# A fused attention and two-MLP kernel: the first eight weight chunks at a lower rank, first operands in one transfer, and another cost of an issue in the schedule

## The chip, the cores and the metric

The kernel runs on one core of a Trainium2 chip. The metric is the device time of one execution in microseconds (us). A core has five engines, each with an instruction queue of its own that it works through in order: TensorE (PE in the profile; PEld is its load of the stationary operand, which runs beside the products), VectorE (DVE), ScalarE (ACT), GpSimd (POOL) and SyncE (SP), which in this kernel does nothing but issue the DMA transfers. An instruction waits on semaphores for the results of other engines and of transfers.

## What is computed

```python
def _attn_ref(q, k, v):                 # B=4, H=8, S=576, D=64
    scores = scale * np.matmul(q, k.transpose(0, 1, 3, 2))
    mask = block_i >= block_j           # blocks of 64 positions
    scores = np.where(mask, scores, -1000000000.0)
    attn = softmax(scores)
    return np.matmul(attn, v)

def _moe_ref(x, w1, w2, w3, w_out):     # x is 2304 x 512, w1..w3 are 512 x 768
    h = np.maximum(np.maximum(x @ w1, x @ w2), x @ w3)
    return h @ w_out

def _moe2_ref(x, w_in, w_out):          # w_in is 512 x 2048
    h = np.maximum(x @ w_in, 0.0)
    return h * h @ w_out

def reference(...):                     # heads are put side by side in between
    return _moe2_ref(_moe_ref(_attn_ref(q, k, v)))
```

q, k and v are 32-bit floats. The weights of both MLPs are 64-bit floats and come to the chip as such.

## The kernel before, in words

**Stages.** The 32 heads are worked on as 16 pairs n (four batches of four pairs, NPAIR = 4). A pair has two groups of query rows, g = 0 (the first 256) and g = 1 (the other 320). For each, TensorE forms scores (sc) from the operands (zk for group 0 of the first four pairs, z and k for their group 1, qs, kh, kl for later pairs), VectorE masks them and takes the negated maximum (nm), ScalarE forms the exponentials (P) with their sums (sm), TensorE transposes them (tp), ScalarE or VectorE copies the transposes out (ta, tb), TensorE multiplies with v (av) and spreads the reciprocal sums over rows (r), which ScalarE copies out (rs). The result, x, is split in two halves of shorter numbers, xh and xl.

The first MLP (`mlp1(b, g)`) multiplies x of one batch and group with w1, w2 and w3, in six columns c of 128 by three i: tiles l, with running maximum run; then h, split in hh and hl, with w_out (also named l, from wo1h and wo1l), copied to ys and written to y_d. Every product is three products of halves: low times high, high times low, high times high. The second MLP follows, in a later stage with other buffers: y is loaded (yf), multiplied with the rearranged second weights wq into ph (p is its copy, c and g the activations), and g with wol and woh into acc.

**Weights.** `load_w_` takes one chunk of 128 rows by 512 numbers: a transfer of 512 KB (raw_w, raw_wo or raw_wi, in 64 bits), two conversions on ScalarE, a shift and a bit operation on VectorE, a sum on GpSimd, a cast to the high half on ScalarE (w1h) and a subtraction on VectorE (w1l). The first MLP has 18 chunks of w1 to w3, named raw_w_c_i, and six of w_out (raw_wo_0 to raw_wo_5). `with_weights` deals them out among the attention steps of batch 0. In the second MLP the chunks become tiles wqf, then wq, which is written to wq_d (1792 KB each) and loaded again later.

**What sets the order.** The code only notes operations. `Plan.issue` then chooses, one at a time, the engine and operation with the earliest start by its own tables of durations (`duration`, `transfer`); of those that could start at the same time on an engine, the one of the lowest rank goes first, then the one noted first. A chunk of the first weights has rank 0 as the attention does, mlp1 has rank 1, the second weights 2. The result is a fixed order on each engine, and on SyncE a fixed order of transfers. There are eight DMA queues used in turn, so an issue also waits for the transfer issued eight before it.

The operands of group 0 of a pair n < 4 are one tile zk of 128 by 3 by 256: z of head 0, z of head 1, and k, brought by three transfers of 128 KB in `score_operands_f32`. Two such tiles exist.

Of the kernel before, what the change touches and what calls it, by code (L numbers as in the profile page):

```python
# [24 lines left out]
NPAIR = H // 2  # L25
# [15 lines left out]
GA, GB = 256, 320  # L41
# [3 lines left out]
CFG = dict(PD=-1, PE=1, A1=0, A2=0, WP=1, FC=(8, 16), WO=55, FI=0, LO2=0, HI2=0, Q2=0, RN=3, XL=2, HL=2, SO=0, TF=0, W_A=0.7, W_B=1.5, SPARE='hl..rhl..rhl..r..r..r', S=15, PB=3, QB=(2, 2, 3), BANKS=(3, 2, 1, 2), LO=0, HI=0, Q=0, EV=('*', '*'), EV2=('a', 'a'), CB=2, PC=0, PM=1000, PX=-0.5, PO=0, HH='*', XH='*', N0='a', YS='a', HIS=0, RB=1, TB=(2, 1), KB=1, CT='a', LT='d', XA=4, XB=0)  # L45
# [123 lines left out]
class Plan:  # L169
# [56 lines left out]
    def issue(self):  # L226

        ops, free, held, queue = self.ops, self.free, self.held, self.queue
        left = [0 for op in ops]
        users = [[] for _ in ops]  # L230
        for op in ops:
            for d in (*op.deps, *op.after):
                if d.end is None:
                    left[op.index] += 1
                    users[d.index].append(op)
        waiting = {e: {} for e in free}

        def offer(op):
            for e in op.engines:
                when = 0.0  # L240
                for d in op.deps:
                    when = max(when, d.end + ((SEM[d.engine] + (500 if e == 'pe' else 0)) if d.engine != e else 0))
                waiting[e][op.index] = when, shares_port(e, op)

        for op in ops:
            if not left[op.index]:
                offer(op)
        for _ in ops:
            best = None
            for e, w in waiting.items():  # L250
                if not w:
                    continue
                other = held["pool" if e == "dve" else "dve"] if e in held else 0.0
                start = {i: max(free[e], at, other if port else 0.0) for i, (at, port) in w.items()}
                t = min(start.values())
                i = min((i for i, s in start.items() if s <= t), key=lambda i: (ops[i].rank, i))
                if best is None or t < best[0]:
                    best = t, e, i
            t, e, i = best
            op = ops[i]  # L260
            op.engine = e
            length = duration(e, op) * SLOW[e]
            if e in held and waiting[e][i][1]:
                held[e] = t + length - HOLD[e]
            for other in op.engines:
                del waiting[other][i]
            if e == "sp":
                queue = max(t + 1500, queue) + transfer(op)
                op.end, free[e] = queue + 400, t + 60
            else:  # L270
                op.end = t + length
                free[e] = op.end - LAP[e]
            for tile in op.makes:
                tile.make()
            self.tc.keep_in_program_order(self.call(self.real[e], alias(e, op.name), op.args, op.kw))
            for u in users[i]:
                left[u.index] -= 1
                if not left[u.index]:
                    offer(u)
        self.ops, self.queue = [], queue  # L280
# [15 lines left out]
def width(x):  # L296
    return math.prod(x.area.shape[1:])


def alias(engine, name):  # L300
    return {"act": "copy", "dve": "tensor_copy"}.get(engine, name) if name in ("copy", "tensor_copy") else name


def shares_port(engine, op):
    if engine not in ("dve", "pool"):
        return False
    sources = [x for k, x in op.kw.items() if k.startswith("in") and isinstance(x, View) and not x.psum]
    if engine == "pool" or len(sources) > 1:
        return bool(sources)
    return bool(sources) and not op.kw["out"].psum and width(op.kw["out"]) % 2 == 0 and op.name != "tensor_reduce"  # L310


def duration(engine, op):
    views = op.views()
    n = max(map(width, views))
    psum = any(x.psum for x in views)
    if engine == "pe":
        stat, mov = op.args[1:] if op.args[1:] else (op.kw["lhsT"], op.kw["rhs"])
        if op.name == "transpose":
            return 109  # L320
        n, m = width(op.args[0]), width(stat)
        if stat.tile.args[1] == F32:
            return (4 * n / 2.4 + 5) * (0.5 if m == 64 else 1)
        return max(n, 230) / 2.4 + (11 if n < 300 else 13)
    if engine == "act":
        if op.name == "activation" and "accum_out" in op.kw:
            return 455 + 0.834 * n
        return (160 if psum else 200) + 0.82 * n
    if engine == "pool":
        return 140 + 2.25 * n  # L330
    if engine == "sp":
        return 60
    if op.name == "memset":
        return 60 + n
    if op.name == "reciprocal":
        return 150 + 6.4 * n
    if op.name in ("tensor_scalar", "tensor_copy", "copy") and not psum:
        return (200 if isinstance(op.kw.get("scalar1"), View) else 150) + n / 1.92
    return 157 + n / 0.96


def transfer(op):
    x = next(v for v in op.views())
    return 128 * 4 * width(x) / 320.0


@with_exitstack
def fused_kernel(ctx: ExitStack, tc: tile.TileContext, z0, k0, qk, v, w123, wo1, win2, wo2, out):
    nc = Plan(tc)
    mm = nc.tensor.matmul  # L350

# [23 lines left out]


    def load_w(src, hi, lo, name):
        with nc.ranked(CFG["PC"]):
            load_w_(src, hi, lo, name)

    def load_w_(src, hi, lo, name, f=None):
# [42 lines left out]
    chunks = []  # L424
# [61 lines left out]
    def score_operands_f32(n, g):  # L486


        a, w = GROUPS[g] if n < NPAIR else (0, S)
        if n < NPAIR and g == 0:  # L490
            zk = at.tile([128, 3, GA], F32, tag="tb", bufs=2 * CFG["TB"][1], name=f"zk{n}")
            z, k = [zk[:, h] for h in range(2)], zk[:, 2]
        else:
            z = [at.tile([128, w], F32, tag=t, bufs=CFG["QB"][2 * (t == "kl")], name=f"z{n}_{t}") for t in ("qs", "kl")]
            k = at.tile([128, S], F32, tag="kh", bufs=CFG["QB"][1], name=f"k{n}")
        nc.sync.dma_start(out=z[0], in_=z0[n, :, 0, a:a + w])
        nc.sync.dma_start(out=k, in_=k0[n, :, :a + w])
        nc.sync.dma_start(out=z[1], in_=z0[n, :, 1, a:a + w])
        return [[(z[h], k)] for h in range(2)], None

    def value_operands(n, g):
# [279 lines left out]
    with nc.behind(marks[CFG["WO"]][0]), nc.ranked(2):  # L781
        for m in (m for q in range(NQ) for m in (q, q + NQ)):
            t = at.tile([128, 2, DM], F32R, tag="wos", name=f"wos{m}")
# [265 lines left out]
```

## Time and profile before

| what | value |
| --- | --- |
| median of 3 runs | 888.12 us (883.44 to 889.05) |
| profiled execution: time | 888.7 us |
| profiled execution: span | 886.9 us |
| mean granted clock of TensorE | 0.995 of full |
| TensorE busy | 864.2 us (97%) |
| VectorE busy | 601.1 us (68%) |
| ScalarE busy | 424.9 us (48%) |
| GpSimd busy | 104.0 us (12%) |

All times in rows come from the profiled execution and count from the start of its span. Busy shares are means over the whole span; the stages differ, so they are read stage by stage.

### The profile page before, as it was taken

How to read it: one execution, taken by the hardware profiler on the slowest of the kernel's cores; microseconds unless marked ns; L12 is line 12 of the kernel's file. 1: busy time of each engine (PE TensorE's matmuls, PEld its weight loads, DVE VectorE, ACT ScalarE, POOL GpSimd, SP SyncE). 2: the span in 40 equal slices, each digit the busy share in tenths (PEclk: the TensorE clock that was granted, in tenths of full speed). 3: DMA queues.
4: the chain of work that ended last, by engine and by line, in shares of the span. 5: the costliest groups of instructions: out<-in, count | busy, mean ns of one | idle time of the engine just before them, and what ended most of it. 6: DMA issues, size and time to landing. Idle time of an engine off the chain costs nothing.

```text
span 886.9 us, 14852 instructions
## 1 busy us (share of the span) xinstructions
PE 864.2 (97%) x5464; PEld 777.7 (88%) x5464; DVE 601.1 (68%) x1376; ACT 424.9 (48%) x1016; POOL 104.0 (12%) x94
## 2 busy tenths in 40 slices
PE   5899999999999999999999989999999999999997
PEld 4567799998999989899999979898999989999896
DVE  6998678878788988646557766546755457544543
ACT  6888667667688787544555231113211114211111
POOL 2233200000001111214442230000000000000000
PEclk9999999999999999999999999999999999999999
DMA  8745432232255563554656578454765536655221
GB/s 294 237 138 174 131 114 89 85 115 86 85 184 177 175 213 118 196 190 165 257 203 237 164 299 338 160 230 168 270 229 184 207 145 229 215 200 196 72 72 71
DMA packets 52056, 157.73 MB, mean 178 GB/s; under 512 B 8592, under 2 KB 16016, under 8 KB 48400
## 3 DMA queue, kind: packets, MB, share of 16 engines
q1 hardware_dynamic: 51984, 156.78, 50.5%
q8 instruction: 43, 0.70, 0.3%
q14 instruction: 29, 0.24, 0.1%
HBM read 124.26 MB, written 32.51 MB: 177 GB/s over the span
## 4 chain that ended last, share of the span: by engine, by line
PE 92%; DVE 2%; DMA 2%; ACT 2%; issue 0%; POOL 0%; SPq 0%; ACTq 0%; POOLq 0%; DVEq 0%
PE l L187 34%; PE acc L187 22%; PE ph_x L187 11%; PE ph_y L187 8%; PE av L187 5%; PE sc L187 5%; PE tp L187 4%; PE sc_t L187 2%; DMA raw_wi<-in_win 1%; PE tp_t L187 1%; DMA raw_wo<-in_wo 1%; DMA zk<-in_k 1%; PE r L187 0%; ACT P L187 0%; DVE f_wo L187 0%
## 5 line engine op out<-in xcount | busy, mean ns | idle before, releaser
L187 PE MATMUL acc<-woh,g 128*128 128x512 f32 x576 | 198.5, 395 | 0.0
L187 PE MATMUL l<-xh,w1l 128*128 128x256 f32 (+1 forms) x576 | 174.3, 303 | 0.9 <-DVE run L187 0.9
L187 PE MATMUL l<-xl,w1h 128*128 128x256 f32 (+1 forms) x576 | 172.2, 299 | 0.0
L187 PE MATMUL l<-xh,w1h 128*128 128x256 f32 (+1 forms) x576 | 172.2, 299 | 0.0
L187 ACT CAST g<-c 128x384 fp32r<-128x384 f32 x96 | 49.3, 513 | 220.8 <-DVE c L187 220.8
L187 PEld LDWEIGHTS acc<-woh,g 128*128 128x128 f32 x576 | 108.5, 189 | 19.4
L187 PE MATMUL acc<-wol,g 128*128 128x512 f32 x288 | 113.3, 393 | 0.0
L187 PEld LDWEIGHTS l<-xh,w1l 128*128 128x128 f32 x576 | 109.0, 189 | 4.1 <-issue 1.5
L187 PEld LDWEIGHTS l<-xl,w1h 128*128 128x128 f32 x576 | 109.1, 189 | 2.6 <-issue 1.7
L187 PEld LDWEIGHTS l<-xh,w1h 128*128 128x128 f32 x576 | 109.1, 189 | 1.9 <-issue 1.2
L187 PE MATMUL ph_x<-t,wq 128*128 128x384 f32 x432 | 87.7, 337 | 2.7 <-ACT p L187 2.7
L187 PEld LDWEIGHTS ph_x<-t,wq 128*128 128x128 f32 x432 | 77.4, 188 | 8.9 <-ACT p L187 3.1
L187 DVE TENSOR_TENSOR g<-c,g 128x384 fp32r<-128x384 f32 x96 | 53.6, 560 | 43.0 <-ACT g L187 42.6
L187 ACT ACTIVATE P<-sc,nm 128x128 f32<-128x128 f32 (+3 forms) x128 | 66.9, 530 | 9.9 <-DVE nm L187 8.4
L187 DVE TENSOR_TENSOR run<-l,run 128x256 f32<-128x256 f32 (+1 forms) x96 | 43.7, 455 | 27.9 <-PE l L187 26.3
L187 POOL TENSOR_TENSOR f_wo<-f_wo,raw_wo 128x512 int32<-128x512 int32 x22 | 29.8, 1357 | 276.5 <-DVE sm L187 180.3
L187 PEld LDWEIGHTS acc<-wol,g 128*128 128x128 f32 x288 | 54.3, 189 | 7.8
L187 PE MATMUL l<-hh,wo1l 128*128 128x256 f32 (+1 forms) x192 | 57.7, 306 | 2.2 <-DVE wo1l L187 2.1
L187 PE MATMUL ph_y<-b,wq 128*128 128x384 f32 x288 | 58.3, 337 | 0.0
L187 PE MATMUL l<-hl,wo1h 128*128 128x256 f32 (+1 forms) x192 | 57.5, 301 | 0.0
L187 PE MATMUL l<-hh,wo1h 128*128 128x256 f32 (+1 forms) x192 | 57.4, 300 | 0.0
L187 DVE TENSOR_REDUCE nm<-sc 128x2 f32<-128x256 f32 (+2 forms) x96 | 55.1, 588 | 0.8
(135 smaller groups left out, 1613.1 us busy)
## 6 DMA issues: line engine op xcount, KB each, us to landing
wq<-wq_d SPq DMA_DIRECT2D x20, 1792.0 KB, 8.6
wq_d<-wq SPq DMA_DIRECT2D x8, 1792.0 KB, 7.7
raw<-in_qk SPq DMA_DIRECT2D x24, 576.0 KB, 3.8
wol<-wo_d SPq DMA_DIRECT2D x48, 256.0 KB, 3.2
woh<-wo_d SPq DMA_DIRECT2D x48, 256.0 KB, 4.8
raw_wo<-in_wo SPq DMA_DIRECT2D x22, 512.0 KB, 3.8
raw_w<-in_w SPq DMA_DIRECT2D x18, 512.0 KB, 5.0
wo_d<-wos SPq DMA_DIRECT2D x16, 512.0 KB, 3.1
```

Of the source, the lines that this page charges most:

```text
L187: return getattr(engine, op_name)(*map(value, args), **{k: value(x) for k, x in kw.items()})
```

## The change

Three things are changed. The first eight weight chunks are noted at rank 0.5 in place of 0, so that an attention step that could start at the same moment goes ahead of them. The three transfers of zk become one of 384 KB from a new array, which the host lays out for the four pairs. And the schedule counts 430 ns in place of 60 ns of SyncE's time for each issue, and 1.4 times the transfer time for what is issued in the first 6 us; it does so by the operation's name, which is the same set of operations. All these change the order that `Plan.issue` finds, on all engines, for the attention and both weights.

```diff
@@ Plan.issue
-            if e == "sp":
-                queue = max(t + 1500, queue) + transfer(op)
-                op.end, free[e] = queue + 400, t + 60
+            if op.name == "dma_start":
+                queue = max(t + 1500, queue) + transfer(op) * (1.4 if t < 6000 else 1)
+                op.end, free[e] = queue + 400, t + 430
@@ fused_kernel
     def load_w(src, hi, lo, name):
-        with nc.ranked(CFG["PC"]):
+        with nc.ranked(0.5 if len(chunks) < 8 else 0):
             load_w_(src, hi, lo, name)
@@ score_operands_f32
-        nc.sync.dma_start(out=z[0], in_=z0[n, :, 0, a:a + w])
-        nc.sync.dma_start(out=k, in_=k0[n, :, :a + w])
-        nc.sync.dma_start(out=z[1], in_=z0[n, :, 1, a:a + w])
+        if n < NPAIR and g == 0:
+            nc.sync.dma_start(out=zk, in_=zk0[n])
+        else:
+            nc.sync.dma_start(out=z[0], in_=z0[n, :, 0, a:a + w])
+            nc.sync.dma_start(out=k, in_=k0[n, :, :a + w])
+            nc.sync.dma_start(out=z[1], in_=z0[n, :, 1, a:a + w])
@@ host
+    zk0 = np.stack([z0[:NPAIR, :, 0, :GA], z0[:NPAIR, :, 1, :GA], k0[:NPAIR, :, :GA]], axis=2)
```

The first place is the start of the program on SyncE. Numbers behind names tell buffers apart; zk_80 belongs to pair 0, the next zk to pair 1, and the last zk shown to pair 2. Before:

```order
L187 DMA zk_80<-in_z 128x256
L187 DMA zk_80<-in_k 128x256
...
L187 DMA v_0_84<-in_v 128x256
L187 DMA raw_w_0_0_86<-in_w 128x1024
L187 DMA zk_88<-in_z 128x256
...
L187 DMA v_0_92<-in_v 128x256 [waits DMAHW0_49]
L187 DMA raw_w_0_1_94<-in_w 128x1024 [waits DMAHW1_49]
...
L187 DMA zk_129<-in_z 128x256 [waits DMAHW6_49,PE_49]
```

In the changed kernel:

```order
L187 DMA zk_80<-in_zk 128x768
L187 DMA v_0_82<-in_v 128x256
L187 DMA zk_84<-in_zk 128x768
...
L187 DMA z_qs<-in_z 128x320
L187 DMA k_90<-in_k 128x576
...
L187 DMA kt_107<-in_k 128x576 [waits DMAHW3_49]
L187 DMA zt_113<-in_z 128x2x64 [waits DMAHW4_49]
L187 DMA raw_w_0_0_116<-in_w 128x1024 [waits DMAHW5_49]
L187 DMA zk_124<-in_zk 128x768 [waits DMAHW6_49,PE_49]
L187 DMA raw_w_0_1_127<-in_w 128x1024 [waits DMAHW7_49]
```

The tile of pair 1 moves from the sixth to eighth issue to the third; the first chunk, raw_w_0_0, moves from fifth to fourteenth, behind the operands of group 1; and the tile of pair 2 from the 23rd to the 15th.

The second place is the start of the program on ScalarE, where P_0_0 and P_1_0 are exponentials of the two steps of a pair's group 0. Before:

```order
L187 ACTIVATE raw_w_0_0_86<-raw_w_0_0_86 128x512 [waits DMAHW4_49]
L187 ACTIVATE P_0_0_138,sm_0_139<-sc_0_0_120,nm_0_127 128x128 [waits DVE_49,PE_49]
...
L187 ACTIVATE P_1_0_149,sm_0_139<-sc_1_0_122,nm_1_135 128x256 [waits DVE_49,PE_49]
...
L187 ACTIVATE raw_w_0_0_86<-raw_w_0_0_86 128x512
L187 ACTIVATE raw_w_0_1_94<-raw_w_0_1_94 128x512 [waits DMAHW1_49]
L187 COPY ta_158<-tp_1_0_161 128x2x256 [waits PE_49]
...
L187 ACTIVATE P_0_0_199,sm_0_200<-sc_0_0_145,nm_0_167 128x128 [waits DVE_49]
```

In the changed kernel:

```order
L187 ACTIVATE P_0_0_119,sm_0_120<-sc_0_0_100,nm_0_110 128x128 [waits DVE_49,PE_49]
...
L187 ACTIVATE P_1_0_133,sm_0_120<-sc_1_0_105,nm_1_122 128x256 [waits DVE_49,PE_49]
...
L187 ACTIVATE P_0_0_161,sm_0_162<-sc_0_0_129,nm_0_144 128x128 [waits DVE_49,PE_49]
...
L187 ACTIVATE P_1_0_172,sm_0_162<-sc_1_0_139,nm_1_164 128x256 [waits DVE_49,PE_49,Activation_49]
...
L187 COPY rs_0_182<-r_0_174 128x256 [waits PE_49]
L187 COPY ta_197<-tp_0_0_189 128x2x128 [waits PE_49]
L187 CAST xh_0_202<-av_0_180 128x256 [waits DVE_49]
...
L187 ACTIVATE raw_w_0_0_116<-raw_w_0_0_116 128x512 [waits DMAHW5_49]
...
L187 ACTIVATE raw_w_0_1_127<-raw_w_0_1_127 128x512 [waits DMAHW7_49]
```

The conversions of the first chunk, which stood ahead of the first exponential, now stand behind the exponentials and copies of two pairs.

The third place is the passage from the first MLP to the second, at the end of `mlp1(3, 1)`, where the last chunks raw_wi are fetched and converted. On SyncE before:

```order
L187 DMA yf_0_6507<-y_d 128x2x768 [waits DMAHW1_49,DVE_49,Activation_49]
...
L187 DMA wol_9_6708<-wo_d 128x512 [waits DMAHW0_49,PE_49]
L187 DMA woh_9_6712<-wo_d 128x512 [waits DMAHW1_49,PE_49]
L187 DMA wq_d<-wq_6387 128x3584 [waits DMAHW2_49,DVE_49]
L187 DMA y_d<-ys_1_3_6724 128x320 [waits DMAHW3_49,Activation_49]
L187 DMA raw_wi_6753<-in_win 128x1024 [waits DMAHW4_49,Pool_49]
L187 DMA raw_wi_6784<-in_win 128x1024 [waits DMAHW5_49,Activation_49,Pool_49]
```

In the changed kernel:

```order
L187 DMA raw_wi_6374<-in_win 128x1024 [waits DMAHW4_49,DMAHW5_49,Activation_49,Pool_49]
L187 DMA wq_d<-wq_6372 128x3584 [waits DVE_49]
L187 DMA yf_0_6531<-y_d 128x2x768 [waits DMAHW2_49,DMAHW6_49,DVE_49,Activation_49]
...
L187 DMA woh_9_6726<-wo_d 128x512 [waits DMAHW2_49,PE_49]
L187 DMA wol_9_6733<-wo_d 128x512 [waits DMAHW3_49]
L187 DMA raw_wi_6738<-in_win 128x1024 [waits DMAHW4_49,Pool_49]
L187 DMA raw_wi_6757<-in_win 128x1024 [waits DMAHW5_49,Pool_49]
L187 DMA wq_d<-wq_6755 128x3584 [waits DMAHW6_49,DVE_49]
```

The transfer wq_d that stood two issues ahead of the last raw_wi now stands ahead of the loads of yf, and the next wq_d comes behind the last raw_wi. On ScalarE at the same passage, before:

```order
L187 COPY ys_1_2_6689<-l_3_1_2_6647 128x320 [waits DMAHW7_49,PE_49,Activation_49]
L187 ACTIVATE wqf_6717<-raw_wi_6370 128x512 [waits DVE_49]
L187 COPY ys_1_3_6724<-l_3_1_3_6679 128x320 [waits DMAHW0_49,PE_49,Activation_49]
L187 ACTIVATE wqf_6717<-raw_wi_6389 128x512
L187 COPY p_0_0_6737<-ph_0_x 128x384 [waits PE_49]
L187 CAST g_0_0_0_6763<-c_0_00_6750 128x384 [waits DVE_49]
...
L187 CAST g_0_1_1_6806<-c_0_11_6794 128x384 [waits DVE_49]
...
L187 CAST g_0_0_1_6831<-c_0_01_6812 128x384 [waits DVE_49]
L187 ACTIVATE raw_wi_6753<-raw_wi_6753 128x512 [waits DMAHW4_49,Activation_49]
...
L187 ACTIVATE wqf_6846<-raw_wi_6784 128x512 [waits DMAHW5_49]
...
L187 COPY p_0_1_6865<-ph_1_x 128x384 [waits PE_49]
```

In the changed kernel:

```order
L187 ACTIVATE wqf_6450<-raw_wi_6338 128x512 [waits DMAHW3_49,Activation_49]
...
L187 ACTIVATE wqf_6450<-raw_wi_6374 128x512 [waits DMAHW4_49]
...
L187 COPY ys_1_3_6715<-l_3_1_3_6676 128x320 [waits DMAHW1_49,PE_49,Activation_49]
L187 COPY p_0_0_6729<-ph_0_x 128x384 [waits PE_49]
...
L187 CAST g_0_0_0_6762<-c_0_00_6744 128x384 [waits DVE_49]
...
L187 ACTIVATE raw_wi_6738<-raw_wi_6738 128x512 [waits DMAHW4_49]
L187 ACTIVATE raw_wi_6757<-raw_wi_6757 128x512 [waits DMAHW5_49]
L187 CAST g_0_1_1_6807<-c_0_11_6787 128x384 [waits DVE_49]
L187 ACTIVATE wqf_6816<-raw_wi_6738 128x512 [waits DVE_49]
...
L187 CAST g_0_0_1_6825<-c_0_01_6804 128x384 [waits DVE_49]
...
L187 COPY p_0_1_6848<-ph_1_x 128x384 [waits PE_49]
```

The conversions of the second-to-last pair into wqf moved ahead of the copies ys, and those of the last pair (raw_wi_6753 and raw_wi_6784 before, raw_wi_6738 and raw_wi_6757 now) moved ahead of the cast g_0_1_1.

## Rows read from the trace of the kernel before

**Rows 1.** The page, busy time of an engine, share of the span, instructions.

```profile
PE 864.2 (97%) x5464; PEld 777.7 (88%) x5464; DVE 601.1 (68%) x1376; ACT 424.9 (48%) x1016; POOL 104.0 (12%) x94
```

**Rows 2.** Stretches of 20 us: length, then PE, PEld, DVE, ACT, POOL busy; PEclk, DMA share, GB/s.

```profile
0.00:20.00 20.00, 11.40 (x60) 7.70 (x60) 11.23 (x31) 12.61 (x34) 4.90 (x9) 1.00 0.89 299
20.00:40.00 20.00, 16.85 (x111) 11.46 (x111) 19.55 (x53) 17.00 (x48) 5.54 (x5) 1.00 0.69 214
40.00:60.00 20.00, 19.59 (x138) 14.41 (x137) 18.51 (x45) 18.21 (x46) 7.63 (x6) 1.00 0.60 197
60.00:80.00 20.00, 20.00 (x138) 14.71 (x137) 17.43 (x42) 17.43 (x45) 6.02 (x5) 1.00 0.46 150
...
500.00:520.00 20.00, 17.30 (x94) 15.88 (x93) 13.33 (x24) 8.28 (x15) 6.52 (x7) 1.00 0.91 338
```

**Rows 3.** Timeline of PE: start, length, instruction, count, idle time before it and releaser.

```profile
3.51 2.90 PE L187 MATMUL sc<-zk 128*128 128x128 f32 x8 [3.51 <-DMA zk<-in_k]
8.41 1.62 PE L187 MATMUL sc<-zk 128*128 128x128 f32 x4 [2.00 <-DMA zk<-in_k]
...
20.63 2.86 PE L187 MATMUL sc<-zk 128*128 128x128 f32 x16 [1.96 <-DMA zk<-in_k]
...
27.29 0.36 PE L187 MATMUL l<-xh,w1l 128*128 128x256 f32 x1
...
106.13 0.39 PE L187 MATMUL l<-hh,wo1l 128*128 128x256 f32 x1 [1.71 <-DVE wo1l L187]
...
519.52 1.50 PE L187 MATMUL ph_x<-t,wq 128*128 128x384 f32 x6 [2.70 <-ACT p L187]
```

**Rows 4.** Timeline of DVE, first step.

```profile
5.65 0.17 DVE L187 MEMSET sc<- 64x128 f32 x1 [4.79 <-PE sc L187]
...
6.59 0.15 DVE L187 TENSOR_SCALAR nm<-nm 128x2 f32<-128x2 f32 x1
```

**Rows 5.** Timeline of ACT, first step and around 510.

```profile
7.57 0.66 ACT L187 ACTIVATE raw_w<-raw_w 128x512 f32<-128x512 f32 x1 [5.35 <-DMA raw_w<-in_w]
8.14 0.35 ACT L187 ACTIVATE P<-sc,nm 128x128 f32<-128x128 f32 x1
...
508.69 0.51 ACT L187 CAST g<-c 128x384 fp32r<-128x384 f32 x1
...
516.67 0.65 ACT L187 ACTIVATE raw_wi<-raw_wi 128x512 int32<-128x512 uint32 x1 [4.05 <-DMA raw_wi<-in_win]
...
519.00 0.47 ACT L187 COPY p<-ph_x 128x384 f32<-128x384 f32 x1
```

**Rows 6.** Pieces of the chain of waits: start, length, what.

```profile
3.54 4.73 DMA zk<-in_k
...
103.40 1.31 POOL f_wo L187
...
507.94 10.06 DMA raw_wi<-in_win
```

**Rows 7.** Stretches of 2 us after the stops at 106 and 519, columns as rows 2.

```profile
108.00:110.00 2.00, 2.00 (x12) 2.00 (x11) 0.76 (x1) 0.09 (x1) 0.00 (x0) 0.50 0.59 152
...
520.00:522.00 2.00, 2.00 (x8) 1.81 (x7) 1.97 (x4) 0.22 (x2) 1.92 (x2) 0.63 0.46 194
522.00:524.00 2.00, 2.00 (x7) 1.62 (x7) 1.41 (x3) 0.35 (x1) 1.32 (x2) 0.52 0.48 141
```

**Rows 8.** Timeline of SP's queue: issues, start and length.

```profile
1.19 0.41 SPq L187 DMA_DIRECT2D zk<-in_k  x1
...
505.08 0.38 SPq L187 DMA_DIRECT2D wq_d<-wq  x1
...
506.26 2.02 SPq L187 DMA_DIRECT2D raw_wi<-in_win  x2
```

**Rows 9.** DMA issues: count, KB each, median us from issue to landing.

```profile
raw_w<-in_w SPq DMA_DIRECT2D x18, 512.0 KB, 5.0
...
k<-in_k SPq DMA_DIRECT2D x4, 288.0 KB, 5.4
```

More of the change, by code (lines that the diff above doesn't have):

```diff
@@ L347, in fused_kernel @@
 @with_exitstack
-def fused_kernel(ctx: ExitStack, tc: tile.TileContext, z0, k0, qk, v, w123, wo1, win2, wo2, out):
+def fused_kernel(ctx: ExitStack, tc: tile.TileContext, z0, zk0, k0, qk, v, w123, wo1, win2, wo2, out):
     nc = Plan(tc)
@@ L1037 @@
     arrays = {
-        "z0": z0, "k0": k0, "qk": qk, "v": vc, "w123": w123, "wo1": w["moe_w_out"], "win2": win2, "wo2": w["moe2_w_out"],
+        "z0": z0, "zk0": zk0, "k0": k0, "qk": qk, "v": vc, "w123": w123, "wo1": w["moe_w_out"], "win2": win2, "wo2": w["moe2_w_out"],
     }
```

## The prediction

> **What bounds the kernel now.** First the page's busy times: TensorE is busy 864.2 of 886.9 us [rows 1], so all idle time of TensorE together is 22.7 us, and no change of order or of transfers can win more than that, apart from time at the lower clock. Next the busy times by stretches of 20 us, read for where these 22.7 us lie [rows 2]: TensorE is busy 11.40 of the first 20 us and 16.85 of the next 20, so 11.75 us of idleness stand in the first 40 us; from 40 to 80 it is 0.41; 2.70 us stand at 500 to 520. The rest is pieces under 2 us, of which the prediction uses one, at 106. In the first 40 us the reader should also see that VectorE is busy 19.55 of 20 us from 20 on and ScalarE 17.00: TensorE is not the engine that sets the pace there.
>
> Then the timeline of the head, engine by engine. TensorE's first score product starts at 3.51, its second group, for head pair 1, at 8.41 after 2.00 us of waiting for zk, and the group of pairs 2 and 3 at 20.63 after 1.96 us of the same wait; the first product of the weights (l) stands at 27.29 [rows 3]. VectorE's first memset on scores is at 5.65, and the scaled maximum (nm) of the first step, on which the exponential depends, starts at 6.59 and takes 0.15 [rows 4]. Yet ScalarE's first exponential P is at 8.14: ahead of it in ScalarE's order stands the conversion of the first weight chunk (raw_w), which starts at 7.57 after 5.35 us of waiting for its transfer [rows 5]. In the chain of waits that head is a transfer too: 4.73 us of zk<-in_k, issued at 3.54 as the seventh transfer [rows 6].
>
> Last the two later stops. At 106.13 TensorE waits 1.71 us for the low half of the last chunk of w_out (wo1l), behind GpSimd's sum at 103.40, and then runs at a granted clock of 0.50 from 108 to 110, that is at 1.2 GHz [rows 3, 6, 7]. At 519.52 it waits 2.70 us for ScalarE's copy p, at 519.00, which stands in ScalarE's order behind raw_wi at 516.67, which had waited 4.05 us for a transfer issued at 507.94 and 10.06 us under way; after that the clock is 0.63 and 0.52 for 4 us [rows 3, 5, 6, 7].
>
> **The profiled execution and the median.** The profiled run took 888.7 us with a span of 886.9, and the median of three is 888.12. The sum is made against 888.7; the two differ by less than the runs do among themselves (883.44 to 889.05), so I take nothing off for it.
>
> **The change, part by part.**
>
> *The first operands in one transfer each.* Twelve transfers of 128 KB become four of 384 KB, eight issues fewer, each 0.41 us in SyncE's queue and 0.47 from one to the next (1.19 to 3.54 for five) [rows 6, 8]. For pair 0: in the kernel before, the middle transfer lands 2.3 us after its issue at 1.19 (the first product starts at 3.51), and the scores of both heads are there for VectorE at 5.65. The trace has no 384 KB transfer. From below, the shortest landing of 128 KB, 2.3 us, puts the tile at 3.0; from above, the 5.4 us of k (288 KB, in a full queue) [rows 9] at 6.1. Nearest is the head itself, with nearly empty queues; I take 3.8, so 4.5. Then both heads follow without a second wait, and VectorE starts at about 4.9 in place of 5.65: 0.7 earlier, between 2.2 earlier and 0.9 later. For pair 1 the tile is the third issue, about 1.7, and lands near 6, so the 2.00 us of waiting at 8.41 go.
>
> The Trainium skill, page "DMA: Bandwidth & Descriptors", section "Anatomy of one DMA", gives a transfer a fixed part of about 2.0 us and a part by bytes over 436 GB/s, fitted on GpSimd's software queues. By it, as an estimate, 128 KB take 2.3 us, which agrees with the 2.3 us of the trace on SyncE's queue, and 384 KB take 2.9; the tile would be there at 3.6, and the head would win 0.9 us more than I put down.
>
> *The first eight chunks behind the attention.* Two things move. On ScalarE the exponentials of pairs 0 and 1 stand first, and with nm ready 1.1 us after VectorE's start, as before (5.65 to 6.74), the first P runs near 6.0 in place of 8.14. On SyncE the first chunk goes from the fifth issue to the fourteenth and waits there for the queue slot of an earlier k (sixth issue, near 3.1; 5.4 us to land); with 5.0 us for itself [rows 9] it is there at about 13.5, so conversion starts some 6 us later than 7.57. Pairs 2 and 3 gain: their zk goes from the 23rd issue to the 15th, and most of the 1.96 us at 20.63 go.
>
> What the head can give to the end is less than what TensorE stops waiting. A chunk costs ScalarE and VectorE the same as before, and both also do the softmax; from 20 to 40 VectorE is idle 0.45 us [rows 2]. So the end of the head, the last wo1l before 106.13, moves only by what these two engines lose less at the start: VectorE 0.7 us, ScalarE about 2.1 (8.14 to 6.0). Were TensorE alone to decide, it would be the 2.00 and the 1.96, 4 us. And if the 6 us of late conversion are not made up by the two engines having done their attention early, it is a loss; I bound that at +3, half of the 6. I take -2.0, the gain of ScalarE, range -4 to +3.
>
> *New order in the middle of the head.* In the order of the changed kernel chunk 2_1 comes late among the weights of its column, and TensorE runs a longer stretch of scores, transposes and values without the l products that filled it. There the trace has only 0.41 us of idleness (40 to 60); the nearest rows of attention without filler are those at 8.41 and 20.63, about 2 us each. Between 0 and +3, I take +0.7: most of the stretch has other attention steps in it.
>
> *The stop at 106.* On all engines the last chunks of w_out are ordered as before, with the sum on GpSimd, the cast and the subtraction in a row, so the stop stays: 0. If TensorE arrives earlier there than the last wo1l does, the stop grows by as much; that is the reason why the head gives only 2.0.
>
> *The stop at 519.* The schedule's new cost of an issue moves transfers far from the head too. In the changed order the conversion of the pair of chunks before the last one stands ahead of the copies ys, and the 1792 KB of wq_d that were issued at 505.08, just ahead of the last pair of raw_wi [rows 8], go out before the loads of yf, long before. GpSimd then has released the buffers long before, so the second raw_wi no longer waits for its sum: both go out near 505 in place of 506.26 and 507.94, with 1.8 MB less in front. With the 10.06 us that it took at most, it is there at 515; with the median of all raw_w, 5.0, at 510. I take 511. Against that, ScalarE now takes raw_wi ahead of one more cast g, so this cast comes at 512 in place of 508.69 [rows 5]; behind it stand two conversions of 0.65, two casts and p, which is then due at about 514.5, and TensorE runs out of work at 516.82 (519.52 less 2.70). So the 2.70 us go. The lower clock costs about half of the time at 0.63 and 0.52, (1-0.63)*2+(1-0.52)*2 = 1.7 us, and goes with the stop. Together -4.4; I keep 0.9 for the cast g that comes later, so -3.5; if the transfer lands as late as now it is 0.
>
> **Sum:** 888.7 - 2.0 + 0.7 + 0 - 3.5 = 883.9 us.
>
> **Rivals.** *Everything falls into place* (chance 0.17): the 4 us of TensorE's waits at the head count in full because VectorE and ScalarE catch up in the 5.1 us that they have idle between 60 and 80 together (twice 20 less 17.43), the stop at 106 goes as well (1.71, and about 1 us of its slow clock), and at 519 the full 4.4: 888.7 - 11.1 = 877.6. Against it: the chain at 103 to 106 is unchanged.
>
> *Nothing is won in the end* (0.18): the head runs into the same last wo1l, and the last raw_wi lands after 515 because eight loads of wol and woh still go out right ahead of it. Then TensorE's waiting is only moved, and the time is 888.
>
> *Weights too late, slower* (0.10): the chunks that start 6 us later stay 6 us later, up to the last one. TensorE finds its l products missing after 30 us and at the latest wo1l at 112 in place of 106: +6, with another 1.7 us at half clock behind a longer stop, and only 0.5 won at 519: 888.7 + 6 + 1.7 - 0.5 = 895.9. It decides from the point where the lag at a chunk exceeds the time by which chunks are ready ahead of their products; for it speaks VectorE's 19.55 of 20, against it that the same engines have the attention of two pairs behind them by then.
>
> A rule on the clock belongs here. The trace shows 0.50 and 0.52 after stops of 1.71 and 2.70 us, but 1.00 through the first 20 us, where TensorE was idle 8.6 us [rows 2]. The Trainium skill, page "TensorE: Matmul & The Clock Gate", section "Part 1: The HAM clock gate", says that the throttled state is the default and activity releases it; by that rule the longer pauses of a thinner attention stretch at 40 to 65 would cost double, and the sum would be about 1.7 us higher. The head of this trace does not bear it out, so it stays with the slower rival.
>
> *The one transfer lands too late*: at 6.1 the first step loses 0.9 us and the head's gain is about 1; this is inside the forecast.
>
> **How the numbers follow.** The forecast has 0.55. Its own range, with -4 to +3 for the head against -2, 0 to +3 for the middle against 0.7, and 0 to -4.4 at 519 against -3.5, is about 880 to 889.5, since the three ends will not meet. The first rival reaches below, to 877.6, the second is inside, the third reaches to 896. I leave out the outer half of the first and most of the third: 878.0 to 891.0. One per cent is 8.9 us, about what a measurement here can tell from no change: faster means under 879.2, slower over 897.0. Faster: most of the first rival and a little of the forecast, 0.18. Slower: the worse end of the third, 0.06. The rest, 0.76, is within 1%.
>
> **What would show it.** In the changed profile: TensorE's second group of scores without a wait near 8.4; the first P near 6.0; the first raw_w on ScalarE near 13.5; the last wo1l between 102 and 105 with TensorE waiting there; TensorE's idle time of the first 40 us 6 to 9 us in place of 11.75; no stop over 1 us between 500 and 525, and the granted clock at 1.00 there. I would be wrong if the last wo1l comes after 108 (then the slower rival), if new waits of TensorE between 40 and 70 sum to more than 3 us, or if raw_wi still lands after 515.

## The result, and the profile after

The changed kernel takes 893.0 us (median of 7 runs, 888.43 to 897.67), the kernel before 885.96 beside it (7 runs): a ratio of 1.0077, 95% interval 1.0049 to 1.0104. It is slower by 0.8%, about 7 us, outside the predicted range on the slow side. The profiled run is at the median (893.0, span 890.7); that of before (888.7) lay 2.7 us above the median of its seven, so the two traces differ by only 3.8 us of span, and sizes are taken from the timed comparisons. Some 0.4 us of the loss lies outside the span: time less span is 2.2 to 2.3 us in every execution of a kernel with the changed kernel's order in the attention and the first MLP, and 1.7 to 1.9 in every other one. What fills it the traces do not show.

The page of the changed kernel, busy times:

```profile
PE 867.0 (97%) x5464; PEld 778.6 (87%) x5464; DVE 602.8 (68%) x1377; ACT 421.0 (47%) x1015; POOL 103.0 (12%) x94
```

TensorE is idle 890.7 - 867.0 = 23.7 us, 1.0 more than by [rows 1], and busy 2.8 us longer with as many instructions, at a mean granted clock of 0.990 in place of 0.995. That adds up to the 3.8, but does not say where the time was lost: a product that runs slower can fill time in which TensorE would have waited. Stretches of 20 us, columns as [rows 2]:

```profile
0.00:20.00 20.00, 11.25 (x69) 7.96 (x69) 11.37 (x34) 10.04 (x33) 1.98 (x7) 1.00 0.93 331
20.00:40.00 20.00, 19.09 (x107) 12.45 (x106) 17.77 (x46) 18.35 (x49) 6.61 (x5) 0.83 0.57 180
40.00:60.00 20.00, 18.77 (x135) 13.66 (x133) 17.47 (x43) 18.77 (x46) 9.42 (x7) 1.00 0.56 185
60.00:80.00 20.00, 19.55 (x139) 14.51 (x139) 16.51 (x44) 16.53 (x41) 6.20 (x6) 1.00 0.45 137
...
500.00:520.00 20.00, 15.60 (x81) 14.39 (x81) 12.44 (x23) 7.37 (x13) 3.43 (x4) 0.90 0.80 293
```

Idle time of the first 40 us fell from 11.75 to 9.66, but the granted clock from 20 to 40 is 0.83 in place of 1.00. From 40 to 80 TensorE idles 1.68 (0.41 before), from 500 to 520 4.40 (2.70). VectorE, 19.55 from 20 to 40 in [rows 2], has 17.77 now. TensorE's timeline, columns as [rows 3]:

```profile
4.03 3.60 PE L187 MATMUL sc<-zk 128*128 128x128 f32 x12 [4.03 <-DMA zk<-in_zk]
...
14.79 1.58 PE L187 MATMUL sc<-zk 128*128 128x128 f32 x8 [0.17 <-DMA zk<-in_zk]
19.71 0.68 PE L187 MATMUL tp<-ident,P 128*128 128x128 f32 x2 [3.34 <-ACT P L187]
...
28.91 0.57 PE L187 MATMUL l<-xh,w1l 128*128 128x256 f32 x1
...
107.82 0.39 PE L187 MATMUL l<-hh,wo1l 128*128 128x256 f32 x1 [2.32 <-DVE wo1l L187]
...
109.21 0.47 PE L187 MATMUL sc<-kh,qs 128*128 128x128 f32 x2 [0.41 <-ACT ys L187]
...
517.16 0.80 PE L187 MATMUL acc<-woh,g 128*128 128x512 f32 x1 [4.40 <-DVE g L187]
```

The two waits of about 2 us for zk are gone. In their place is one of 3.34 before 19.71, for pair 2's exponential. The last wo1l comes at 107.82 (106.13), and the late stop is longer, 4.40, and ends on another operation. VectorE and ScalarE in the head, and ScalarE at 515:

```profile
5.34 0.17 DVE L187 MEMSET sc<- 64x128 f32 x1 [4.48 <-PE sc L187]
...
16.50 0.43 DVE L187 TENSOR_SCALAR raw_w<-raw_w 128x512 int32<-128x512 int32 x1
16.96 0.69 DVE L187 SCALAR_TENSOR_TENSOR raw_w<-raw_w 128x512 int32<-128x512 int32 x1
...
18.33 0.77 DVE L187 TENSOR_SCALAR nm<-nm 128x2 f32<-128x2 f32 x1
```

```profile
6.27 0.37 ACT L187 ACTIVATE P<-sc,nm 128x128 f32<-128x128 f32 x1 [4.04 <-DVE nm L187]
...
15.79 1.78 ACT L187 ACTIVATE raw_w<-raw_w 128x512 f32<-128x512 f32 x3
...
19.20 0.37 ACT L187 ACTIVATE P<-sc,nm 128x128 f32<-128x128 f32 x1 [1.62 <-DVE nm L187]
...
514.22 0.67 ACT L187 ACTIVATE raw_wi<-raw_wi 128x512 int32<-128x512 uint32 x1 [6.01 <-DMA raw_wi<-in_win]
...
516.02 0.49 ACT L187 CAST g<-c 128x384 fp32r<-128x384 f32 x1
```

The first chunk, 8.2 us later on ScalarE than at 7.57 in [rows 5], meets pair 2's scores on VectorE: its two steps (16.50 and 16.96) go ahead of pair 2's maximum, and P waits for that until 19.20. At 514 the cast g stands behind raw_wi, which waited 6.01 us. SyncE's issue of the last two raw_wi, and one piece of the chain of waits:

```profile
507.42 1.32 SPq L187 DMA_DIRECT2D raw_wi<-in_win  x2
```

```profile
508.06 7.38 DMA raw_wi<-in_win
```

Stretches of 2 us behind the three stops:

```profile
22.00:24.00 2.00, 2.00 (x12) 1.34 (x13) 1.60 (x4) 2.00 (x5) 1.30 (x1) 0.50 0.64 148
24.00:26.00 2.00, 2.00 (x12) 1.24 (x11) 1.65 (x5) 2.00 (x6) 1.11 (x1) 0.50 0.32 127
...
110.00:112.00 2.00, 2.00 (x10) 2.00 (x11) 1.37 (x5) 0.67 (x4) 0.00 (x0) 0.50 0.61 62
...
518.00:520.00 2.00, 2.00 (x6) 1.63 (x6) 2.00 (x6) 0.63 (x2) 0.00 (x0) 0.50 0.88 344
```

With 20 to 22 (0.74) and 26 to 28 (0.55), the clock from 20 to 28 falls 3.4 us short of full ((1-0.74)x2 and so on); before it was 1.00 there. Whether this costs any time is another question, which e4, e11 and e13 put.

### The profile page after: what moved, and what is told of

It reads as the page before. It is cut to its first block, busy times and chain, and to the rows that moved or that the text cites. A ratio compares the mean times of both kernels' runs of the same rounds, so it can differ in the third digit from the quotient of the medians.

```text
span 890.7 us, 14828 instructions
## 1 busy us (share of the span) xinstructions
PE 867.0 (97%) x5464; PEld 778.6 (87%) x5464; DVE 602.8 (68%) x1377; ACT 421.0 (47%) x1015; POOL 103.0 (12%) x94
## 4 chain that ended last, share of the span: by engine, by line
PE 92%; DMA 2%; DVE 2%; ACT 2%; issue 1%; POOL 0%; SPq 0%; DVEq 0%; POOLq 0%; ACTq 0%
PE l L187 33%; PE acc L187 22%; PE ph_x L187 11%; PE ph_y L187 8%; PE av L187 5%; PE sc L187 5%; PE tp L187 4%; PE sc_t L187 2%; DMA raw_wi<-in_win 1%; PE tp_t L187 1%; PE r L187 1%; DMA wo_d<-wos 1%; DMA raw<-in_qk 0%; DMA zk<-in_zk 0%; ACT raw_w L187 0%
## 5 line engine op out<-in xcount | busy, mean ns | idle before, releaser
L187 PE MATMUL tp<-ident,P 128*128 128x128 f32 x320 | 52.7, 278 | 5.0 <-ACT P L187 4.7
```

What stands on the lines that cost most here:

```text
L187: return getattr(engine, op_name)(*map(value, args), **{k: value(x) for k, x in kw.items()})
```

## The experiments

All were timed in five rounds beside the kernel before (885.94 to 886.06 in the four groups); ratios are to it, with 95% intervals. "Stage 1" is what the first call of `Plan.issue` orders (the attention and most of the first MLP), "stage 2" the second call (the rest of the first MLP, and the second). For e1 to e3, e6, e7 and e12 an order of engine and operation was written down for a stage (counted from 0 in the code) and replayed in place of the planner's choice (in e12 one list per engine):

```diff
+            if script:                      # ORDER[stage], if there is one
+                i, e = next(script)
+                e = ("pe", "dve", "act", "pool", "sp")[e]
+                best = max(free[e], waiting[e][i][0]), e, i
```

**e1, transfers alone** (order of before in both stages).

> The four zk tiles come in one transfer each, and every engine keeps the order of the kernel before, in both stages. Theory A (the loss sits in the new order: a new stop of TensorE at 16 to 20 us with half clock behind it, and a longer stop at 512 with half clock behind it): the transfers alone cost nothing and win at most the 2.00 and 1.96 us of waiting for zk, 883 to 887 us. Theory B (late weight chunks set the end of the head, through the last low half of w_out): same time as before, 885 to 887, since the chunks are not later here; TensorE then waits longer than 1.71 us for the last chunk. If the transfers themselves are the loss: 890 or more.

887.67 us, 1.0016 [0.9999, 1.0034]. The first product starts at 4.00 in place of 3.51, and the gain at pair 2 is given back in a wait for ScalarE behind it:

```profile
20.12 2.89 PE L187 MATMUL sc<-zk 128*128 128x128 f32 x16 [1.00 <-DMA zk<-in_zk]
...
26.21 0.82 PE L187 MATMUL tp<-ident,P 128*128 128x128 f32 x2 [2.55 <-ACT P L187]
```

The transfers win nothing by themselves, and the time lies in none of the three ranges. In the old order, with chunks no later in it, the last wo1l comes 1.70 later than before:

```profile
107.83 0.39 PE L187 MATMUL l<-hh,wo1l 128*128 128x256 f32 x1 [1.70 <-DVE wo1l L187]
```

**e2, new stage 1 with the old stage 2.** Edit: `ORDER = {1: order of before}` in the changed kernel.

> The first stage (attention, w1, w_out, up to about 400 us) in the order of the changed kernel, with the one transfer per tile; the second stage in the order of the kernel before. Theory A: the stop at 512 goes back to 2.7 us and its clock loss to 1.7, so 889.5 to 891, about 3 less than the changed kernel, still slower than before by the head's clock loss. Theory B: the head alone makes the loss, 892 to 894.

890.56 us, 1.0046 [1.0032, 1.006]: the stop in the head is there (3.57 before 20.39, then clock 0.50 from 20 to 26), the last wo1l at 108.02. The time is within Theory A's range.

**e3, old stage 1 with the new stage 2.** Edit: `ORDER = {0: order of before, 1: order of after}` in the kernel before.

> The first stage as in the kernel before, three transfers per tile included; the second stage in the order of the changed kernel. Theory A: 888 to 889.5, slower than before by the longer stop at 512 (1.7 us of waiting and about 1 of clock). Theory B: as before, 885 to 887.

887.75 us, 1.0011 [0.9994, 1.0028], between the two ranges and not told apart from no change. Its stop is 3.24 us before 513.63, for DVE g. The first stage carries the larger part of the loss, and stage 2 wins nothing.

**e4, the stop of the head filled.** Products that nobody reads keep TensorE busy; 26 transposes of the identity stand ahead of pair 2's first transposes.

```diff
+            if FILL.get(op.makes[0].kw["name"] if op.makes else None):
+                for _ in range(FILL[op.makes[0].kw["name"]]):
+                    self.tc.keep_in_program_order(self.call(self.real[e], op.name, (op.args[0], op.args[2], op.args[2]), op.kw))
...
+FILL = {'tp2_0_0': 26}
```

> The changed kernel with 26 idle transposes of the identity ahead of pair 2's first transposes, so that TensorE works during its stop at 16.4 to 19.7; they write a tile that is overwritten before it is read. Theory A: the granted clock stays at 1.00 from 20 to 28 and 2 to 3.4 us are won: 889.5 to 891. Theory B: the clock stays high too, but the last low half of w_out comes at 107 as before and TensorE waits there for what it won, 892 to 894.

889.61 us, 1.0042 [1.0028, 1.0057]. Timeline and stretches of e4:

```profile
20.00 0.68 PE L187 MATMUL tp<-ident,P 128*128 128x128 f32 x2 [0.36 <-ACT P L187]
...
22.00:24.00 2.00, 1.84 (x11) 1.18 (x11) 1.46 (x4) 2.00 (x6) 1.26 (x1) 0.54 0.52 105
24.00:26.00 2.00, 2.00 (x12) 1.39 (x12) 1.91 (x5) 2.00 (x5) 0.85 (x2) 0.61 0.42 172
```

The stop is 0.36 in place of 3.34, though pair 2's exponential is no earlier; the clock is low only from 22 to 26, which is 1.7 us short of full. By its median the kernel is about 3 us faster than the changed one (892.66 in e5 below), as Theory A has it. The trace has Theory B's sign, though: TensorE's first product of the weights and the last wo1l stand where they stand in e5, behind the same wait. Lines of e4, then of e5:

```profile
28.01 0.58 PE L187 MATMUL l<-xh,w1l 128*128 128x256 f32 x1
...
107.06 0.39 PE L187 MATMUL l<-hh,wo1l 128*128 128x256 f32 x1 [2.32 <-DVE wo1l L187]
```

```profile
28.01 0.57 PE L187 MATMUL l<-xh,w1l 128*128 128x256 f32 x1
...
106.90 0.39 PE L187 MATMUL l<-hh,wo1l 128*128 128x256 f32 x1 [2.32 <-DVE wo1l L187]
```

What the higher clock won there was gone by 28 us. Where the 3 us of the median are won stays open: the one trace of e4 is of its longest execution (891.43).

**e5, the changed kernel again, e6, the rank alone, e7, the cost alone** (e6 and e7 are the kernel before with that line and a replayed stage 2 of before).

> The changed kernel as it is, beside the runs that follow, so that its time is known from the same chip in the same hour. The run with the filled stop took 889.6 us and the one with the old second stage 890.6. If the filled stop won what its clock promised, this one stays near 893 (Theory A); if VectorE and ScalarE set the pace of the head whatever TensorE's clock does (Theory C: the late chunks cost 1 to 3 us at the last w_out chunk), the fill won nothing and this one is at 889 to 891.

892.66 us, 1.0077 [1.0057, 1.0096].

```diff
-        with nc.ranked(CFG["PC"]):
+        with nc.ranked(0.5 if len(chunks) < 8 else 0):
```

> The kernel before with the rank of the first eight chunks at 0.5 alone (three transfers per tile, the old cost of an issue); the second stage keeps the order of the kernel before. The first chunk is then the 18th issue. Theory C: late conversion, so the last low half of w_out comes 1 to 3 us later than 106.1 and the time is 888 to 891. Theory A: a new stop over 3 us near 16 to 20, half clock behind it, 889 to 890. If the rank does no harm, 884 to 886 and the loss is made by the cost of an issue.

892.2 us, 1.0071 [1.005, 1.0093].

```diff
-                queue = max(t + 1500, queue) + transfer(op)
-                op.end, free[e] = queue + 400, t + 60
+                queue = max(t + 1500, queue) + transfer(op) * (1.4 if t < 6000 else 1)
+                op.end, free[e] = queue + 400, t + 430
```

> The kernel before with the new cost of an issue alone in the first stage (rank 0, three transfers per tile); the second stage keeps the order of the kernel before. The first chunk stays the fifth issue, and the first two exponentials go ahead of its conversion on ScalarE. Theory C: conversion starts within 2 us of 7.57, so no loss: 884 to 886, with the first exponential near 7. If the cost of an issue makes the loss by the other moves in the order: 889 or more.

891.62 us, 1.0064 [1.0041, 1.0086]. TensorE's wait in e6, and its first l in e7, which stands at 27.29 in [rows 3]:

```profile
21.52 4.85 PE L187 MATMUL sc<-zk 128*128 128x128 f32 x16 [6.02 <-DMA zk<-in_k]
```

```profile
33.48 0.57 PE L187 MATMUL l<-xh,w1l 128*128 128x256 f32 x1
```

The rank alone and the cost alone each lose about as much as all three parts together; for the rank that is more than any range above. They do not add up: each re-plans the head into another order, with its own late work (the wait of 6.02 for pair 2's operands in e6, the first l 6.2 us later in e7). In e7 the first chunk stays the fifth issue and its conversion starts at 8.63, 1.1 us later than before, and still the last wo1l comes at 109.15 (109.84 in e6): a late first chunk is not needed for the loss.

**e8, the kernel before with the last two chunks planned late.** The schedule takes them to land 6 us later, so their conversions come later in ScalarE's order; no transfer is moved on purpose.

```diff
+                if isinstance(op.kw["out"], View) and op.kw["out"].tile.kw["name"] in ("raw_wi_11", "raw_wi_3"):
+                    op.end += 6000
```

> The kernel before, in which the schedule counts 6 us more for the landing of the last two chunks raw_wi, so that their conversions stand behind the copy p and the casts g on ScalarE; nothing else in the schedule's rules changes, and the order is that of before up to that place. If the stop at 519 is made by the copy behind the waiting conversion, the 2.70 us and 1.7 us of clock go: 881.5 to 883.5. If it only moves (another instruction then waits for the same chunks), 885 to 886.

882.16 us, 0.9955 [0.994, 0.9971]. ScalarE, then the stretch from 500, of e8:

```profile
513.10 0.48 ACT L187 COPY p<-ph_x 128x384 f32<-128x384 f32 x1 [1.85 <-PE ph_x L187]
```

```profile
500.00:520.00 20.00, 20.00 (x109) 18.86 (x108) 15.78 (x30) 8.51 (x16) 6.49 (x6) 1.00 0.92 347
```

The copy p no longer stands behind a conversion that waits, and stop and slow clock are gone: 3.8 us.

**e9, the same in the changed kernel.**

> The changed kernel, in which the schedule counts 6 us more for the landing of the last two chunks raw_wi (the edit that took the kernel before from 886 to 882.2). If the loss is the sum of two places, the stop at 512 (4.4 to 4.8 us and its clock) goes here and the head's loss stays: 886.5 to 889, that is 4.5 to 6.5 above the kernel before with the same edit. If the head loses nothing by itself, 882 to 884.

888.24 us, 1.0016 [0.9998, 1.0035]: 4.4 below the changed kernel (stop 0.50), still 6.1 above e8. So the stop near 515 costs the changed kernel only 0.6 more than the one at 519 costs the kernel before.

**e10, e8 with 14 transposes ahead of the first product with the last wo1l.**

> The kernel before with the same edit, and 14 transposes of the identity into a spare bank ahead of the first product with the last chunk of w_out, so that TensorE works during its stop of 1.71 us at 104.4 to 106.1 and waits no shorter. If the clock behind the stop costs what the rows show (1.7 us between 106 and 112), 880 to 881 in place of 882.2, with a granted clock of 1.00 there; if VectorE and ScalarE set the pace there, 882 to 883.

881.91 us, 0.994 [0.9921, 0.9959], between its two ranges: clock 1.00 up to 878, but not told apart from e8.

**e11, e9 with 28 and 19 transposes** in the head and ahead of the last wo1l.

> The changed kernel with the same edit and with both stops of the first stage filled: 28 transposes ahead of pair 2's first transposes, 19 ahead of the first product with the last chunk of w_out. Nothing else moves. Theory A (the head's loss is the clock behind stops that became longer): 882 to 884, level with the kernel before with the same edit. Theory C (the head's loss is late conversion): 886 to 888, the fills win under 1 us.

885.43 us, 0.9993 [0.9974, 1.0011], again between its ranges; up to 880 the clock was low only at 22 to 28.

**e12, the first chunk behind pair 2.** In the changed kernel its VectorE steps go behind pair 2's maxima and its cast behind the exponentials.

> The changed kernel with three instructions moved in the head, nothing else: on VectorE the shift and the bit operation of the first chunk go behind the maxima of both steps of pair 2, on ScalarE the cast of that chunk behind pair 2's exponentials. If the stop of 3.3 us at 16.4 is made by the first chunk's conversion standing ahead of pair 2's maximum, it falls to 1 to 2 us and the time to 889 to 891; with the clock staying at 1.00 from 20 to 28, to 888 to 889. If the stop is the way from scores to exponentials by itself, it stays over 2.5 us and the time at 892 to 893.

892.88 us, 1.0066 [1.004, 1.0092]. The first stop falls to 1.82, as it was to do, but a second one of 2.21 opens behind it and the time stays:

```profile
18.73 0.68 PE L187 MATMUL tp<-ident,P 128*128 128x128 f32 x2 [1.82 <-ACT P L187]
...
23.45 1.12 PE L187 MATMUL r<-ident,sm 128*64 128x128 f32 x8 [2.21 <-DVE sm L187]
```

**e13, e9 with 32, 8 and 19 transposes.**

> The run with both stops filled, with 32 transposes in place of 28 ahead of pair 2's first transposes and 8 more ahead of the second step's, where the row of that run still had stops of 0.56, 0.76 and 0.29 us and the granted clock fell to 0.50 at 24 to 26. If the rest of the head's loss is the clock, it is 1.00 there now and the time 883 to 884. If the rest is the pace of VectorE and ScalarE, it stays at 885 to 886, with the last low half of w_out near 107.5 as before.

884.84 us, 0.9977 [0.9964, 0.9991], just under the second range, with clock 1.00 up to 879. It is 3.4 below e9, but the two traces are level at the last wo1l and part behind it, where e9 ran at 0.50 from 108 to 114. TensorE's last wo1l and ScalarE's fifth copy ys of e9, then of e13:

```profile
106.95 0.38 PE L187 MATMUL l<-hh,wo1l 128*128 128x256 f32 x1 [2.31 <-DVE wo1l L187]
...
184.34 0.45 ACT L187 COPY ys<-l 128x320 f32<-128x320 f32 x1
```

```profile
107.18 0.38 PE L187 MATMUL l<-hh,wo1l 128*128 128x256 f32 x1 [0.25 <-DVE wo1l L187]
...
182.46 0.45 ACT L187 COPY ys<-l 128x320 f32<-128x320 f32 x1
```

Against e10, which like it has no slow clock up to 878, 2.9 us are left. Stretches of e10, then of e13:

```profile
40.00:60.00 20.00, 19.60 (x138) 14.30 (x137) 18.49 (x45) 18.20 (x46) 7.25 (x6) 1.00 0.56 185
60.00:80.00 20.00, 20.00 (x139) 14.75 (x139) 17.47 (x43) 17.44 (x44) 6.20 (x5) 1.00 0.45 150
```

```profile
40.00:60.00 20.00, 18.77 (x136) 13.56 (x135) 17.55 (x41) 18.86 (x46) 9.71 (x7) 1.00 0.56 184
60.00:80.00 20.00, 19.55 (x141) 14.49 (x140) 15.89 (x44) 16.59 (x40) 6.55 (x5) 1.00 0.42 128
```

VectorE does 2.5 us less from 40 to 80, and TensorE waits 1.7 us there on ScalarE's attention steps (before 55.38, 58.57 and 61.46). VectorE makes part of it up from 80 to 100 and is 2.0 us of work behind at 100. The last wo1l is 1.7 later (107.18 against 105.45).

**e14, e10 with VectorE slowed**: four subtractions into w1l are done twice, with the same result.

```diff
+            if self.stage == 0 and i in TWICE:
+                self.tc.keep_in_program_order(self.call(self.real[e], op.name, op.args, op.kw))
```

> The kernel before with the late planning and the filled stop (881.9 us), in which VectorE does the subtraction for the low half of four chunks (w1_1_0 to w1_2_0) twice, with the same result: 4 by 0.69 to 0.8 us, 2.8 to 3.2 us more of VectorE between 20 and 45. If VectorE sets the pace up to the last chunk of w_out (Theory C), that chunk's low half comes 2 to 3 us later than 105.5 and the time is 883.5 to 885.5. If TensorE alone sets the pace behind the head (Theory A), 882 to 883.

883.71 us, 0.9977 [0.9961, 0.9992], 1.8 above e10. TensorE's last wo1l, and VectorE's first doubled subtraction and the first single one behind them:

```profile
107.81 0.39 PE L187 MATMUL l<-hh,wo1l 128*128 128x256 f32 x1 [0.19 <-DVE wo1l L187]
```

```profile
22.25 1.40 DVE L187 TENSOR_TENSOR w1l<-f_w,w1h 128x512 fp32r<-128x512 f32 x2
...
44.75 0.69 DVE L187 TENSOR_TENSOR w1l<-f_w,w1h 128x512 fp32r<-128x512 f32 x1
```

The same two in e10:

```profile
22.46 0.68 DVE L187 TENSOR_TENSOR w1l<-f_w,w1h 128x512 fp32r<-128x512 f32 x1
...
42.39 0.69 DVE L187 TENSOR_TENSOR w1l<-f_w,w1h 128x512 fp32r<-128x512 f32 x1
```

In the traced execution of e14 TensorE's clock was at 0.50 from 14 to 22, but that did not hold VectorE up: it comes to the first doubled subtraction 0.21 earlier than in e10, is 2.36 behind after the last one, and the last wo1l is late by the same 2.36. The time is in the range for VectorE's pace, though the spans of the two traces are only 0.9 apart.

## Why the prediction was wrong

**The first step, nearly right.** The first product at 4.03 (4.5 taken), VectorE at 5.34 (4.9), the first P at 6.27 (6.0), the pair-1 wait gone, idle time of the first 40 us 9.66 (forecast 6 to 9). The tile landed 3.3 us after its issue at 0.74. The estimate of 2.9 us worked out from the Trainium skill, page "DMA: Bandwidth & Descriptors", section "Anatomy of one DMA", is 0.4 short of that; nothing in the sum rested on it.

**The head, -2.0: the step that failed first.** ScalarE's earlier start was taken as a gain at the last wo1l. The first conversion came at 15.79, not 13.5, and wo1l at 107.82 in place of 102 to 105: 1.7 later than before, not 2.0 earlier (106.90 to 108.02 in the eight traces with the changed first stage). That the late conversion might be "a loss; I bound that at +3, half of the 6" was in the text, but not taken. What the runs show in its place: the last wo1l is set by VectorE's pace. In e14 some 3 us of added work there moved it by 2.36 and the time by 1.8. Each part alone puts it later too (107.83 in e1, 109.84 in e6, 109.15 in e7). Which of VectorE's steps lose the time in the changed order was not isolated; its lag of 2 us at 100 (e13 against e10) is of the right size.

The stop of 3.34 us before 19.71 and the half clock behind it, which I had priced only in the slower rival and at another place, look like the cause, but the traces do not bear that out. With the stop filled the last wo1l stays where it was (107.06 in e4 and 107.18 in e13; 106.90 in e5 and 106.95 in e9). Nor does the clock in the head matter in the old order: e3 and e8 have the same first stage, e3 ran at 0.50 from 22 to 24 and e8 at 1.00, and the last wo1l stands at 105.98 and 106.02. Moving the first chunk does not help (e12).

**The middle of the head, +0.7: a little too small.** TensorE's idle time from 40 to 80 went from 0.41 to 1.68, 1.3 more (the waits from 55 to 62; attention stands there without filler), below the +3 bound.

**The clock in the first 12 us: a wrong reading.** [rows 2] gives 1.00 for the first 20 us, and from that the prediction set a rule aside. But the trace's record of the clock begins only at 11.9 us in the kernel before and at 7.3 in the changed one, and time without a record is printed as 1.00. The products themselves show the rate: until then those of one form (128x128, f32) start 0.213 us apart, afterwards 0.109. A transpose in the kernel before, then one in the changed kernel:

```profile
10.46 0.42 PE L187 MATMUL tp<-ident,P 128*128 128x128 f32 x1
```

```profile
8.01 0.27 PE L187 MATMUL tp<-ident,P 128*128 128x128 f32 x1
```

So TensorE's first products run at half rate, the lower level of 1.2 GHz, in all 16 traces, until 6.5 to 12.3 us. The rule set aside is that of the Trainium skill, page "TensorE: Matmul & The Clock Gate", section "Part 1: The HAM clock gate": the throttled state is the default and activity releases it. The traces agree with it in these first products, and behind the stop at 19.71: 0.50 for 4 us, 1.00 again from 28 after TensorE had been busy throughout. The price that I drew from it, at 40 to 65, did not come: the clock is 1.00 there.

**The stop at 106, 0: too small.** It went from 1.71 to 2.32, with waits of 0.41 for ys and 0.23 for kl right behind it. In the traces of e4, e5 and e9 the clock behind it was 0.50 from 108 to 114; in the kernel before only from 108 to 110, with 0.87 and 0.77 beside.

**The stop at 519, -3.5: the other failed step.** Both raw_wi were to go out near 505, land at 511 and free the cast g at 512. They went out from 507.42 and the last landed at 508.06 + 7.38 = 515.44. TensorE was taken to run out of work at 516.82; in the changed order the products of that g come earlier, and it ran out at 517.16 - 4.40 = 512.76. So the cast that I allowed to come "later" is the one waited for, at 516.02. e8 and e9 show the price: without the wait both kernels win, 3.8 and 4.4.

**Together.** The loss is about 7 us (6.7 and 7.0 in two measurements). 0.6 to 1.0 come from the later stop (6.1 are left between e9 and e8). Some 3 go when both stops of the first stage are filled (3.4 between e13 and e9, with 0.3 for the like fill of e10 against e8); in the two traces none of that is there at the last wo1l, 1.9 at the fifth ys. 2.9 stay with clean clocks (e13 against e10): in the traces the last wo1l is 1.7 later and the span 1.6 longer (881.9 and 880.3), and 0.4 is outside the span; the rest is not found. Open is why e4, which fills the head's stop alone, is 3 us faster by its median. e2 and e3, one stage at a time, give 0.46% and 0.11% of the 0.77%; the rest is within their intervals.

The base of the sum was off as well: 888.7 lies 2.7 above the median of seven. Against the base the forecast was a change of -4.8, and +7.0 was measured, so the forecast time (883.9) looks nearer to 893.0 than the forecast change is.

None of the rivals was it: "weights too late" (895.9, chance 0.10) had the sign and the later wo1l (112; measured 107.82), but not the place of the slow clock. Of the three warning signs named, only the last came true: raw_wi at 515.44; wo1l stayed just short of 108, and the waits from 40 to 70 below 3 us. The best kernels found are e8 and e10, at 882.2 and 881.9, without any of the three parts of this change.

## What to carry to other kernels

Before a wait is priced, find what sets the next point at which the engine has to wait anyway. Here TensorE's idle time in the head fell by 2 us and the kernel lost time; filling a stop of 3.3 us and clearing the half clock behind it left the next such point, the last wo1l, where it was, because VectorE sets it. Where a schedule is planned, a guessed landing time decides what queues behind a waiting conversion on an in-order engine; planning two transfers 6 us later won 3.8 us without touching the work. A re-planned head has to be judged by when its busiest helper engine delivers the last operand that TensorE waits for, and replaying the old order stage by stage tells which part of a re-plan matters.

## What the hardware showed unexpectedly

The granted clock does not follow from one stop alone. With the same order at 106, e1 kept 1.00 behind a wait of 1.70 and e3 fell to 0.50 behind one of 1.72; e2 kept 1.00 behind 2.38 us at 522. In e14 the clock fell inside the first 20 us, behind waits of 1.33, 0.66 and 0.85; the kernel before, with waits of 2.00 and 0.84 in its head, was at 1.00 from 12 us on. A stretch of 2 us of e14:

```profile
14.00:16.00 2.00, 1.29 (x6) 0.56 (x8) 1.68 (x7) 1.58 (x5) 0.00 (x0) 0.50 1.07 381
```

So the gain of one removed stop differs from execution to execution, and is best read from medians.
